# Output products of 128 tokens each, wider filler products, two subtractions moved to VectorE, and a new rank table

## The chip, the core and the metric

The kernel runs on one NeuronCore of a Trainium2 chip. The core has TensorE (PE in the profile; its weight loads are PEld), VectorE (DVE), ScalarE (ACT), GpSimd (POOL) and SyncE (SP), which here issues every transfer. The metric is the device time of one execution in microseconds (us), the median of several runs.

## The reference

Attention between 512 tokens and 32 state rows for 8 x 8 heads, then a gated feed-forward layer on 4352 tokens, then a soft mixture of experts over the same tokens.

```python
scores = scale * np.matmul(x, state.transpose(0, 1, 3, 2))     # x: (8, 8, 512, 64), state: (8, 8, 32, 64)
a = softmax(scores); xread = np.matmul(a, state)
a2 = softmax(scale * np.matmul(state, x.transpose(0, 1, 3, 2))); sread = np.matmul(a2, x)
t = np.concatenate([xread, sread], axis=2)                     # -> (4352, 512) tokens
h = t @ w_in; t = (h * sigmoid(h)) @ w_out                     # 512 -> 2048 -> 512
logits = t @ phi                                               # 32 slots = 8 experts x 4
d = softmax(logits, axis=0); slot_input = d.T @ t
slot_out[e] = np.maximum(slot_input[e] @ w1[e], 0) @ w2[e]     # 512 -> 1024 -> 512 per expert
out = softmax(logits, axis=1) @ slot_out                       # (4352, 32) @ (32, 512)
```

`moe_w_in` and `moe_w_out` arrive as 8-byte floats and are turned into 4-byte floats on the chip.

## The kernel before

The tokens are worked in nine blocks: k = 0 to 7 are the batches (512 tokens of `xread` each), k = 8 (`NB`) is the 256 tokens of `sread`.

The **front** loads `w_in` and `w_out` as sixteen 1 MB halves (`raw`), in the order of the list `RAW`. `conv` turns one half into 4-byte floats: ScalarE takes the high words (`win` or `acc`), ScalarE or, for the halves in `LOW_DVE`, VectorE the low words (`part`), VectorE shifts the high words, GpSimd adds the two. From `w_out` and `phi` the front makes `w2p` (`wo_half`: products `w2ps` and `w2q`). The attention of a block is `a_scores` (product `sc`), `a_split`, `a_soft1` to `a_soft3` (VectorE and ScalarE; from block 2 on GpSimd takes two of the steps), `a_eT` and `a_sread` (`sr`). `a_soft3` ends with `ar`, the attention weights split in a rounded part and a rest, so that fast products give the accuracy of 4-byte floats. `wb(u)` multiplies the state of a block with a quarter of `w_in` (u = 4 * block + quarter) and splits the result in the same way: ScalarE copies the rounded part, and the rest is a subtraction on VectorE, or, for one of its two halves (`WB_POOL`) when u > 3, on GpSimd after a second copy by ScalarE into `wf`.

For each block the **middle** runs `hid` sixteen times (product `h`, ScalarE's or VectorE's gate `g`, a transpose into `blk`), `logits` (`lg`), `s_rep`, `s_norm` and `s_dTg` (`S`), while the attention and the `wb` of later blocks run beside it. The **tail** multiplies the slots with `w_out` (`siaT`, `sia`, `sibT`, `sib`, `siT`), then with the experts' `w1` (`f`) and `w2` (`so`); both arrive in 32 transfers of 1 MB into places that earlier tiles leave. The output is made in two halves of 256 columns: `so` and `sor` of one half, then `out_tiles` for each block. `out_tiles(q, cols, tags)` runs 32 x 32 products of 256 columns (16 for a block of 512 tokens), four output banks with four token groups each; VectorE and ScalarE copy two banks each to `obuf`, and SP stores them (512 KB for a block and half). The first half of the output stands between the products `so` of the second half. Block 7 is made last, with 512 columns at once. A 4-byte product is two instructions on TensorE, each with its weight load.

The order is not that of the code. `Recorder` collects all operations (all have line 504 in the profile), and `schedule` simulates the engines with the costs of `cost`: on each engine it takes the operation that can start first, and among those that can start together the one with the smallest number, which is the position in the code plus an entry of `RANK`. A key of `RANK` is the zone ("0": all that stands ahead of block 1, "m": blocks 1 to 6, "7", "8"), the engine, the operation, the tile's name and a running number. Operations with `op.port` are not put beside each other on VectorE and GpSimd. All loads of the start are ready at once, so that their order is that of the numbers. The numbers of the code for these are: `raw` 0: 1, first state load `ss` 0: 2, `xT` 0: 3, `raw` 1: 4, `cst`: 5, `phi`: 6, `raw` 2: 7, `xk` 0: 8, second state load `ss` 1: 9, `raw` 3 to 7: 10 to 14. `raw` 0 and 1 are the two halves of the first quarter of `w_in`; `xT` 0, `xk` 0 and each `raw` are 1024 KB, `ss` 0 is 64 KB and `ss` 1 448 KB.

Where the simulation leaves TensorE idle in a stretch of `FILL`, `schedule` puts in products whose result nobody reads (`filler`); in the profile they carry the name of the tile whose bank they use, with both operands from `ss` (or `cst`), as `lg<-ss`.

Of the kernel before, what the change touches and what calls it, by code (L numbers as in the profile page):

```python
# [7 lines left out]
F32 = mybir.dt.float32  # L8
# [8 lines left out]
NSLOT = 32  # L17
# [24 lines left out]

EVICT = 100

FILL = ((0.0, 60.0), (380.0, 400.0))
FILLER = (0.47, 0.3)

HALVES = (0, 1, 2, 3, 4, 5, 6, NB)

# [3 lines left out]


RANK = {
    ("0", "ACT", "activation", "acc", 0): 54,
    ("0", "ACT", "activation", "acc", 4): -236,
    ("0", "ACT", "activation", "e", 1): -37,
    ("0", "ACT", "activation", "g", 5): 426,
    ("0", "ACT", "activation", "g", 6): 75,  # L60
    ("0", "ACT", "activation", "g", 10): 427,
    ("0", "ACT", "activation", "g", 14): 358,
    ("0", "ACT", "activation", "g", 15): 60,
    ("0", "ACT", "activation", "part", 3): -128,
    ("0", "ACT", "activation", "part", 7): 683,
    ("0", "ACT", "activation", "win", 0): -53,
    ("0", "ACT", "copy", "wb", 8): 61,
    ("0", "ACT", "copy", "ws", 2): 290,
    ("0", "DVE", "tensor_scalar", "acc", 1): -75,
    ("0", "DVE", "tensor_scalar", "acc", 2): -74,  # L70
    ("0", "DVE", "tensor_scalar", "asm", 2): -164,
    ("0", "DVE", "tensor_scalar", "part", 2): 96,
    ("0", "DVE", "tensor_scalar", "tm", 1): 25,
    ("0", "DVE", "tensor_scalar", "win", 1): -340,
    ("0", "DVE", "tensor_scalar", "win", 3): -51,
    ("0", "DVE", "tensor_scalar", "win", 4): -98,
    ("0", "DVE", "tensor_tensor", "s", 3): 343,
    ("0", "DVE", "tensor_tensor", "wb", 1): 659,
    ("0", "DVE", "tensor_tensor", "wb", 2): 26,
    ("0", "DVE", "tensor_tensor", "wb", 3): 120,  # L80
    ("0", "DVE", "tensor_tensor", "wb", 4): 132,
    ("0", "DVE", "transpose", "blk", 9): -82,
    ("0", "DVE", "transpose", "blk", 11): 399,
    ("0", "PE", "matmul", "h", 12): -436,
    ("0", "PE", "matmul", "wps", 3): 54,
    ("0", "SP", "dma_start", "cst", 0): 40,
    ("0", "SP", "dma_start", "phi", 0): 373,
    ("0", "SP", "dma_start", "raw", 1): -6,
    ("0", "SP", "dma_start", "raw", 2): 53,
    ("0", "SP", "dma_start", "raw", 4): -134,  # L90
    ("0", "SP", "dma_start", "raw", 6): 656,
    ("0", "SP", "dma_start", "ss", 0): -262,
    ("0", "SP", "dma_start", "ss", 1): 118,
    ("0", "SP", "dma_start", "xT", 0): -349,
    ("0", "SP", "dma_start", "xk", 0): 142,
    ("7", "ACT", "copy", "wb", 2): 68,
    ("7", "ACT", "copy", "wf", 1): 77,
    ("7", "DVE", "scalar_tensor_tensor", "g", 0): 253,
# [19 lines left out]
    ("8", "PE", "transpose", "hT", 2): -503,  # L118
    ("8", "PE", "transpose", "lT", 0): 485,
    ("8", "SP", "dma_start", "blk", 10): 66,  # L120
    ("m", "ACT", "activation", "e", 0): 327,
    ("m", "ACT", "activation", "e", 1): -87,
    ("m", "ACT", "activation", "s", 0): 433,
    ("m", "ACT", "activation", "sums", 0): 783,
    ("m", "ACT", "activation", "thb", 2): -393,
    ("m", "ACT", "copy", "e", 0): 449,
    ("m", "ACT", "copy", "wb", 3): 366,
    ("m", "DVE", "reduce_sum", "cm", 0): 365,
    ("m", "DVE", "tensor_copy", "acc", 2): -172,
    ("m", "DVE", "tensor_scalar", "cm", 0): 376,  # L130
    ("m", "PE", "matmul", "S", 0): -413,
    ("m", "PE", "matmul", "h", 11): 276,
    ("m", "PE", "matmul", "lg", 10): -96,
    ("m", "PE", "matmul", "wbp", 2): -647,
    ("m", "PE", "transpose", "eT", 1): 283,
    ("m", "PE", "transpose", "srT", 0): 248,
}

# [36 lines left out]
class Recorder:  # L175
# [90 lines left out]
    def cost(self, op, eng, what, outs, ins, kwargs):  # L266
# [11 lines left out]
        if eng == PE:  # L278
            lhs, rhs = kwargs.get("lhsT"), kwargs.get("rhs")
            if what == "transpose":  # L280
                op.mode, op.tail = FULL, 0.2
                op.cost += 0.11
                return
            rows, cols = list(lhs.ap)[0][1], n(lhs)
            op.mode = (128 if rows > 64 else 64 if rows > 32 else 32, 128 if cols > 64 else 64 if cols > 32 else 32)
            N = n(rhs)
            if op.mode == FULL:
                split = rhs.dtype == F32R
                op.cost += N / 2.4e3 + 0.0157 if split else max(0.2, 4 * N / 2.4e3 + (0.021 if N > 256 else 0.04))
                op.tail = 0.165  # L290
            else:
                tiles = (128 // op.mode[0]) * (128 // op.mode[1])
                m = 2 * len(op.calls)
                op.cost = max(m / tiles * 2 * N / 2.4e3, m * 0.0135) + (0.07 if tiles == 16 else 0.0068 * tiles - (0.02 if N == 128 else 0.0))
                op.tail = 0.165
        elif eng == ACT:
            f = kwargs.get("func")
            base = 0.833e-3 * most
            if f in (AF.Abs, AF.Sign, AF.Relu):
                lat = base + (0.26 if pin else 0.29)  # L300
            elif most == 1024 and outs[0].dtype == U32:
                lat = 1.256
            elif f == AF.Prelu:
                lat = 1.165
            elif len(ins) > 1:
                lat = base + (0.258 if pin else 0.285)
            else:
                lat = base + (0.16 if pin else 0.205)
            if kwargs.get("accum_out") is not None:
                op.cost, op.tail = lat + 0.096, 0.0  # L310
            else:
                op.cost, op.tail = lat - 0.105, 0.105
            op.mode = {AF.Exp: "e", AF.Silu: "s", AF.Tanh: "es"}.get(f)
        elif eng == DVE:
            sb = [kwargs[x] for x in ("in0", "in1") if x in kwargs and kwargs[x].space == bass.MemoryType.SB]
            fast = not pin and not pout and not strided and what in ("tensor_scalar", "tensor_copy")
            op.port = len(sb) > 1 or fast
            if what == "transpose":
                lat = 0.165 + most / 0.96e3
            elif what == "reciprocal":  # L320
                lat = 0.165 + max(0, most - 4) * 6.7e-3
            elif fast:
                lat = 0.262 + most / 1.92e3
            else:
                lat = (0.205 if pin and len(ins) > 2 else 0.155) + most / 0.96e3
            op.cost, op.tail = lat - 0.08, 0.0 if fast else 0.08
        elif eng == POOL:
            lat = 0.2 + most * 2.135e-3
            if most == 1024:
                lat = {F32R: 2.39, U32: 2.5}.get(outs[0].dtype, 1.94)  # L330
            op.cost, op.tail = lat - 0.042, 0.042
        else:
            b = 4
            for s, c in list(outs[0].ap):
                b *= c
            op.bytes = b
            op.cost = 0.42
# [19 lines left out]
    def schedule(self):  # L357
# [38 lines left out]
        while n_left:  # L396
# [42 lines left out]
                free[tag] = f  # L439
                qpos[tag] += 1  # L440
            if e == PE and any(lo < busy[PE] < hi for lo, hi in FILL):
                n = int((st - busy[PE] - 0.3) / FILLER[min(fills, 1)])
                room = []
                for tag in free:
                    if tag.split("_")[1] == "ps" and tag[0] != "h" and (tag[0] == "w" or busy[PE] < 100) and free[tag] and qpos[tag] < len(queue[tag]):
# [44 lines left out]
    def filler(self, name, old, n, start):  # L490


        op = Op()
        op.eng, op.kind, op.firsts, op.done, op.mode, op.start, op.cost = PE, "fill", [name], False, FULL, start, 0.2 * n
        out, v = self.tiles[name][:, 0:128], self.filling[start > 100]
        op.calls = [(self.tc.nc.tensor.matmul, (out,), dict(lhsT=v, rhs=v, start=True, stop=True))] * n
        op.prio, op.idx, op.tail, op.key, op.old = 0, 0, 0.0, None, old
        return op

    def issue(self):  # L500
# [39 lines left out]
def tile_state_attention_soft_moe(  # L540
# [40 lines left out]
    r4 = cst[:, 128:160]  # L581
    masks = cst[:, 256:258]
    ss = unit("ss", [2, 4 * NB * NSLOT], "ss")
    nc.filling = ss[:, 0, 0:128], ident
    st_sb = ss[:, 0, :].rearrange("p (b c n) -> p b c n", b=NB, c=4)
    srT = ss[:, 1, :].rearrange("p (c y x n) -> p c y x n", c=4, y=2, x=4)
    w2p = one.tile([128, 4, 4, NSLOT], F32, tag="w2p", name="w2p")
# [188 lines left out]
    def a_soft3(b):  # L776
# [2 lines left out]
        nc.vector.transpose(out=t, in_=s[:, 0].rearrange("p h t -> p (h t)"))  # L779
        at[b, "ar"] = a = unit("A", [2, 2, 512], f"ar{b}", F32R)  # L780
        nc.scalar.copy(out=a[:, 0], in_=s[:, 1])
        (nc.gpsimd if b else nc.vector).tensor_tensor(out=a[:, 1], in0=s[:, 1], in1=a[:, 0].bitcast(F32), op=ALU.subtract)

    def a_eT(b, h2):
        e = at[b, "e"]
# [33 lines left out]
    def wb_mm(u, cols, n):  # L819
# [13 lines left out]
        for h2 in range(2):  # L833
            q = p[h2][:, :n]
            nc.scalar.copy(out=w[:, 0, h2, cols], in_=q)
            on = nc.vector
            if h2 in WB_POOL and u > 3:
                q = rot.tile([128, 512], F32, tag="wf", name=f"wf{u}_{h2}", bufs=1)[:, :n]
                nc.scalar.copy(out=q, in_=p[h2][:, :n])
                on = nc.gpsimd  # L840
# [582 lines left out]
    def out_tiles(q, cols, tags):  # L1423
# [2 lines left out]
        p = [bank(t, f"o{q}_{cols.start}_{x}") for x, t in enumerate(tags)]  # L1426
        nt = ntok(q) // 128
        with nc.together():
            for y in range(nt):
                for x in range(4):  # L1430
                    m = NSLOT * (4 * q + y)
                    mm(
                        p[x][32 * y:32 * y + 32, :n],
                        lhsT=cT[32 * x:32 * x + 32, m:m + 32],
                        rhs=sor[32 * x:32 * x + 32, cols],
                        start=True,
                        stop=True,
                    )
        for x in range(4):
            r = slice(0, 32 * nt)  # L1440
            (nc.scalar.copy if x % 2 else nc.vector.tensor_copy)(out=obuf[q][r, x, cols], in_=p[x][r, :n])
# [91 lines left out]
```

## Time and profile before

| | before |
|---|---|
| median of 3 runs | 461.36 us (460.88 to 461.5) |
| the profiled execution | 460.03 us, of which its span 456.7 us |
| TensorE busy | 427.5 us, 94% of the span |
| VectorE, ScalarE, GpSimd busy | 311.5, 276.9, 136.7 us |
| granted TensorE clock, mean | 0.992 of full speed |
| the chain that ended last | 82% on TensorE |
| transferred | 92.23 MB, of these 12.06 MB written |

The span runs from the first to the last instruction; the 3.3 us between it and the time of the execution lie around it. Busy shares are means over the stages named above, which have different limits, so that each stage is read by itself: the transfers are at their full rate up to 50 us and again from about 360 us on, and TensorE is busy without a gap in between.

### The profile page before, as it was taken

The numbers are of one execution on the slowest core, as the hardware profiler recorded it, in microseconds if no ns is written. First come the engines' busy times: TensorE is split into PE (matmuls) and PEld (weight loads), VectorE is DVE, ScalarE is ACT, GpSimd is POOL, SyncE is SP. The second block draws the span as 40 slices with busy tenths as digits, with TensorE's granted clock in tenths as the row PEclk, the third lists the DMA queues.
The fourth block names the chain that finished last, engine by engine and source line by source line (L and its number), as shares of the span: only waits on it lengthen the run. The fifth ranks groups of instructions, "written<-read, shape, count | busy, mean of one in ns | idle before, by whom it ended". The sixth has DMA issues, their size and how long they took to land.

```text
span 456.7 us, 12765 instructions
## 1 busy us (share of the span) xinstructions
PE 427.5 (94%) x5584; PEld 272.8 (60%) x5584; DVE 311.5 (68%) x535; ACT 276.9 (61%) x492; POOL 136.7 (30%) x75
## 2 busy tenths in 40 slices
PE   4778999999999999999999999999999999899981
PEld 3555656747656764865775677477577785434430
DVE  2979988888687696788768769767874405212361
ACT  3988987756676495496758649566568423110261
POOL 0746777242133134124214313421146430000000
PEclk9899999999999999999999999999999999999998
DMA  8999931220502412141160223210395899999998
GB/s 323 426 419 385 359 108 72 93 78 30 218 4 93 151 82 95 46 187 25 71 231 3 93 99 134 95 46 3 109 368 204 331 383 423 414 425 427 399 341 284
DMA packets 22247, 92.23 MB, mean 202 GB/s; under 512 B 1712, under 2 KB 9776, under 8 KB 13744
## 3 DMA queue, kind: packets, MB, share of 16 engines
q1 hardware_dynamic: 22192, 91.43, 51.9%
q8 instruction: 43, 0.70, 0.6%
q14 instruction: 12, 0.10, 0.1%
HBM read 79.37 MB, written 12.06 MB: 200 GB/s over the span
## 4 chain that ended last, share of the span: by engine, by line
PE 82%; ACT 6%; DVE 5%; issue 2%; POOL 1%; DMA 1%; DVEq 0%; SPq 0%; ACTq 0%
PE h L504 41%; PE lg L504 8%; PE S L504 8%; PE wbp L504 6%; PE so L504 3%; PE f L504 3%; PE o L504 3%; PE sc L504 2%; PE sr L504 2%; ACT part L504 1%; PE eT L504 1%; DMA ss<-in_stT_dram 1%; ACT e L504 1%; PE dT L504 1%; ACT win L504 1%
## 5 line engine op out<-in xcount | busy, mean ns | idle before, releaser
L504 PE MATMUL h<-ar,wb 128*128 128x512 f32 x768 | 191.0, 400 | 2.5 <-ACT g L504 1.0
L504 PEld LDWEIGHTS h<-ar,wb 128*128 128x128 f32 x768 | 139.8, 188 | 46.7 <-issue 12.5
L504 DVE STREAM_TRANSPOSE blk<-g 128x512 f32<-128x512 f32 x128 | 88.4, 700 | 22.0 <-ACT g L504 21.6
L504 ACT ACTIVATE g<-h 128x512 f32<-128x512 f32 x100 | 59.5, 604 | 55.2 <-PE h L504 35.7
L504 POOL TENSOR_TENSOR wb<-wf,wb 128x512 fp32r<-128x512 f32 x28 | 37.2, 1328 | 143.2 <-ACT wf L504 87.9
L504 PEld LDWEIGHTS lg<-g,w2p 128*32 128x32 f32 x1152 | 29.2, 109 | 28.3 <-issue 14.8
L504 PE MATMUL lg<-g,w2p 128*32 128x128 f32 x1152 | 40.8, 276 | 0.5 <-ACT w2p L504 0.5
L504 PE MATMUL S<-blk,dT 32*32 32x512 f32 (+1 forms) x1040 | 38.5, 599 | 0.4 <-ACT dT L504 0.4
L504 ACT CAST wb<-wbp 128x512 fp32r<-128x512 f32 x64 | 35.5, 597 | 3.4 <-PE wbp L504 3.4
L504 PE MATMUL wbp<-win,ss 64*32 64x512 f32 x512 | 33.7, 606 | 3.2 <-POOL win L504 3.2
L504 POOL TENSOR_TENSOR s<-s,tm 128x1024 f32<-128x1024 f32 x12 | 23.3, 1938 | 28.6 <-DVE tm L504 17.8
L504 POOL TENSOR_TENSOR win<-win,part 128x1024 uint32<-128x1024 uint32 x8 | 20.9, 2614 | 24.8 <-DVE asm L504 16.3
L504 ACT ACT_TABLE_LOAD x21 | 26.9, 1283 | 1.1 <-PEq L1523 0.7
L504 DVE TENSOR_TENSOR wb<-wbp,wb 128x512 fp32r<-128x512 f32 x36 | 24.2, 676 | 2.5 <-ACT wb L504 2.4
L504 DVE SCALAR_TENSOR_TENSOR acc<-acc,m,S 128x512 f32<-128x512 f32 x28 | 19.2, 743 | 7.5 <-PE S L504 7.5
L504 POOL TENSOR_TENSOR wlo<-win,whi 128x1024 fp32r<-128x1024 f32 x8 | 19.0, 2392 | 13.3 <-ACT whi L504 13.3
L504 POOL TENSOR_TENSOR acc<-acc,part 128x1024 uint32<-128x1024 uint32 x8 | 19.5, 2435 | 7.4 <-DVE acc L504 4.9
L504 POOL TENSOR_TENSOR ar<-s,ar 128x1024 fp32r<-128x1024 f32 x7 | 16.8, 2407 | 14.8 <-ACT ar L504 14.8
L504 PE MATMUL h<-whi,rd 128*128 128x512 f32 x64 | 20.5, 401 | 0.0
L504 DVE SCALAR_TENSOR_TENSOR g<-thb,h 128x512 f32<-128x512 f32 x28 | 18.5, 674 | 1.8 <-ACT thb L504 1.8
L504 ACT ACTIVATE thb<-h 128x512 f32<-128x512 f32 x30 | 17.5, 601 | 3.3 <-PE h L504 2.8
L504 DVE TENSOR_REDUCE tm<-s 128x32 f32<-128x1024 f32 x16 | 19.2, 1198 | 0.4 <-ACT s L504 0.4
(161 smaller groups left out, 589.3 us busy)
## 6 DMA issues: line engine op xcount, KB each, us to landing
place<-in_w_dram SPq DMA_DIRECT2D x17, 1024.0 KB, 10.8
blk<-in_w_dram SPq DMA_DIRECT2D x13, 1024.0 KB, 10.0
xT<-in_xT_dram SPq DMA_DIRECT2D x8, 1024.0 KB, 5.0
raw<-in_w_in_dram SPq DMA_DIRECT2D x8, 1024.0 KB, 11.7
raw<-in_w_outT_dram SPq DMA_DIRECT2D x8, 1024.0 KB, 7.8
xk<-in_xk_dram SPq DMA_DIRECT2D x8, 1024.0 KB, 5.0
blk<-in_w_out_dram SPq DMA_DIRECT2D x6, 1024.0 KB, 4.8
out_dram<-place SPq DMA_DIRECT2D x10, 512.0 KB, 5.9
```

The source lines that it names most:

```text
L504: made = [call(*args, **kwargs) for call, args, kwargs in op.calls]
```

## The change

Five edits. (1) `out_tiles` makes each output bank with one product of up to 128 tokens in place of four of 32. (2) Fillers are 256 columns wide in place of 128, stand only in the first 60 us, and their number comes from another formula (2.2 us are taken off the first gap, 0.2 us off the others); both operands come from the first 256 columns of the state tile. (3) The rests of `wb` for u = 4 and 5, and the rest of `ar` for block 1, are subtracted by VectorE; the copies into `wf` of these two u fall away. (4) The planner's costs: a VectorE shift or scaling of 4-byte integers with a strided operand now counts as short and as a user of `op.port`; GpSimd's integer addition counts 2.4 us in place of 2.5. (5) `RANK` has new entries for the zones "0" and "m".

```diff
-FILL = ((0.0, 60.0), (380.0, 400.0))
-FILLER = (0.47, 0.3)
+FILL = ((0.0, 60.0),)
+FILLER = 0.45
...
 RANK = {
...
-    ("0", "SP", "dma_start", "cst", 0): 40,
-    ("0", "SP", "dma_start", "phi", 0): 373,
-    ("0", "SP", "dma_start", "raw", 1): -6,
-    ("0", "SP", "dma_start", "raw", 2): 53,
-    ("0", "SP", "dma_start", "raw", 4): -134,
-    ("0", "SP", "dma_start", "raw", 6): 656,
-    ("0", "SP", "dma_start", "ss", 0): -262,
-    ("0", "SP", "dma_start", "ss", 1): 118,
-    ("0", "SP", "dma_start", "xT", 0): -349,
-    ("0", "SP", "dma_start", "xk", 0): 142,
...
+    ("0", "SP", "dma_start", "cst", 0): 24,
+    ("0", "SP", "dma_start", "phi", 0): 842,
+    ("0", "SP", "dma_start", "raw", 1): -66,
+    ("0", "SP", "dma_start", "raw", 4): 408,
+    ("0", "SP", "dma_start", "raw", 6): 19,
+    ("0", "SP", "dma_start", "raw", 7): 17,
+    ("0", "SP", "dma_start", "xk", 0): 402,
...
-            fast = not pin and not pout and not strided and what in ("tensor_scalar", "tensor_copy")
+            low = strided and outs[0].dtype == U32
+            fast = not pin and not pout and (low or not strided) and what in ("tensor_scalar", "tensor_copy")
             op.port = len(sb) > 1 or fast
...
-                lat = {F32R: 2.39, U32: 2.5}.get(outs[0].dtype, 1.94)
+                lat = {F32R: 2.39, U32: 2.4}.get(outs[0].dtype, 1.94)
...
-                n = int((st - busy[PE] - 0.3) / FILLER[min(fills, 1)])
+                n = int((st - busy[PE] - (0.2 if fills else 2.2)) / FILLER)
...
-        out, v = self.tiles[name][:, 0:128], self.filling[start > 100]
-        op.calls = [(self.tc.nc.tensor.matmul, (out,), dict(lhsT=v, rhs=v, start=True, stop=True))] * n
+        out, v = self.tiles[name][:, 0:256], self.filling
+        op.calls = [(self.tc.nc.tensor.matmul, (out,), dict(lhsT=v[:, 0:128], rhs=v, start=True, stop=True))] * n
...
-    nc.filling = ss[:, 0, 0:128], ident
+    nc.filling = ss[:, 0, 0:256]
...
-        (nc.gpsimd if b else nc.vector).tensor_tensor(out=a[:, 1], in0=s[:, 1], in1=a[:, 0].bitcast(F32), op=ALU.subtract)
+        (nc.gpsimd if b > 1 else nc.vector).tensor_tensor(out=a[:, 1], in0=s[:, 1], in1=a[:, 0].bitcast(F32), op=ALU.subtract)
...
-            if h2 in WB_POOL and u > 3:
+            if h2 in WB_POOL and u > 5:
...
-            for y in range(nt):
-                for x in range(4):
-                    m = NSLOT * (4 * q + y)
-                    mm(
-                        p[x][32 * y:32 * y + 32, :n],
-                        lhsT=cT[32 * x:32 * x + 32, m:m + 32],
+            for x in range(4):
+                m = 4 * NSLOT * q
+                mm(
+                    p[x][0:32 * nt, :n],
+                    lhsT=cT[32 * x:32 * x + 32, m:m + 32 * nt],
```

## Rows read from the trace of the kernel before

**Rows 1.** The page: rate of transfers in 40 slices of 11.4 us; instruction loads (packets, MB).

```profile
GB/s 323 426 419 385 359 108 72 93 78 30 218 4 93 151 82 95 46 187 25 71 231 3 93 99 134 95 46 3 109 368 204 331 383 423 414 425 427 399 341 284
...
q8 instruction: 43, 0.70, 0.6%
```

**Rows 2.** Stretches: length, busy time of each engine, clock, transfer share, GB/s.

```profile
20.00:49.90 29.90, 25.58 (x265) 18.16 (x257) 27.11 (x35) 26.69 (x37) 17.65 (x7) 0.96 1.01 406
49.90:66.00 16.10, 15.62 (x140) 9.91 (x140) 14.46 (x21) 13.95 (x21) 12.67 (x5) 1.00 0.57 207
60.00:80.00 20.00, 19.57 (x218) 11.49 (x217) 17.61 (x20) 15.42 (x27) 14.31 (x7) 1.00 0.16 56
```

**Rows 3.** TensorE in order of time, 6 to 20 us: start, length, operation, idle before.

```profile
6.17 1.96 PE L504 MATMUL sc<-xT,ss 64*32 64x512 f32 x16 [6.17 <-DMA ss<-in_stT_dram]
...
18.56 1.70 PE L504 MATMUL wbp<-win,ss 64*32 64x512 f32 x16 [2.97 <-POOL win L504]
```

**Rows 4.** The chain that ended last, 0 to 66 us: start, length, piece.

```profile
11.19 0.60 DVE win L504
...
12.78 1.06 ACT win L504
...
14.54 1.15 ACT part L504
...
18.94 0.56 DVE win L504
...
20.63 2.79 DVE acc L504
...
31.78 2.18 issue
```

**Rows 5.** Operations by tile: VectorE on the low words; ns min/median/max, first and last.

```profile
L504 DVE TENSOR_SCALAR part<-raw x6: 676/2034/2870, 31.2 to 66.0; 128x1024 uint32<-128x1024 uint32 x6
```

**Rows 6.** Operations by tile: the subtractions that VectorE does already.

```profile
L504 DVE TENSOR_TENSOR wb<-wbp,wb x36: 645/680/692, 23.3 to 333.8; 128x512 fp32r<-128x512 f32 x36
...
L504 DVE TENSOR_TENSOR ar<-s,ar x1: 1211/1211/1211, 26.5 to 26.5; 128x1024 fp32r<-128x1024 f32 x1
```

**Rows 7.** The chain that ended last, 420 to 457 us.

```profile
424.09 0.66 PE o L504 x32
424.74 1.44 PE so L504 x24
...
430.96 0.68 issue
...
436.73 0.73 PE o L504 x16
...
440.80 1.05 issue
...
446.53 1.16 issue
...
448.89 0.67 DVE place L504
```

**Rows 8.** Stretches of the output phase, columns as in rows 2.

```profile
435.00:441.00 6.00, 5.05 (x176) 2.42 (x177) 4.00 (x12) 3.63 (x12) 0.00 (x0) 1.00 0.96 312
441.00:450.00 9.00, 5.35 (x146) 1.62 (x145) 4.81 (x12) 4.35 (x12) 0.00 (x0) 1.00 1.08 378
450.00:452.00 2.00, 0.00 (x0) 0.00 (x0) 0.16 (x1) 0.00 (x0) 0.00 (x0) 1.00 0.94 267
```

**Rows 9.** Weight loads in order of time: start, length of the group, operation.

```profile
421.92 0.24 PEld L504 LDWEIGHTS o<-thb,place 32*32 32x32 f32 x32 [0.92 <-DVE thb L504]
...
125.58 0.42 PEld L504 LDWEIGHTS dT<-cst,d 128*128 128x128 f32 x4 [0.84 <-ACT thb L504]
```

**Rows 10.** TensorE beside the fillers: the stretch after its longest idle time; 386 to 392 us.

```profile
19.00:22.00 3.00, 3.00 (x24) 1.81 (x9) 3.00 (x3) 2.58 (x4) 2.42 (x1) 0.50 1.01 415
...
389.14 0.67 PE L504 MATMUL sibT<-thb,r4e 64*32 64x128 f32 x32 [1.13 <-DVE fin L504]
```

## What the change should do to the time, before it is measured

> **What bounds the kernel now.** I read the slices of the page first. They show three stages. Up to about 57 us the transfers run at 323 to 426 GB/s, then they drop, and from the 33rd slice (365 us) on they are above 380 GB/s again until the output begins [rows 1]. Next come the stretches. Before 49.9 us TensorE is busy 25.58 of 29.9 us, a good part of it with fillers; ScalarE is busy 26.69 and VectorE 27.11 of the 29.9: the conversions and the first attention set the pace. From 49.9 to 66 us TensorE is busy 15.62 of 16.1, and so it stays to the tail [rows 2]. A microsecond won before 49.9 us is thus handed through whole, since block after block the rest hangs on TensorE; a microsecond won on another engine after 49.9 us is worth nothing. Third, the chain of waits in the front: the pieces I want are those in which VectorE works or waits for something that is not the attention itself [rows 4]. Last, the chain in the output phase, where TensorE's products `o` and `so` alternate and TensorE three times stands still with "issue", waiting for nothing that the profile shows [rows 7], and the transfer rate in the same microseconds [rows 8].
>
> **The output products.** A full tile is now 32 instructions and takes 0.66 us of the chain, a round of `so` with 24 instructions 1.44, that is 0.48 for the eight instructions of four products side by side [rows 7]. The new tile is eight instructions, four products side by side, each on its own 32 rows and into its own bank. I price it like `so`, at 0.48, since both stream 256 columns four at a time; 0.18 less for each of eight tiles is 1.4 us between the first `o` and the last `so`.
>
> The three "issue" pieces are 0.68, 1.05 and 1.16 us [rows 7]. I take them for instructions that come late: 43 loads carry TensorE's 11168 instructions [rows 1], 260 each. From the first output tile on TensorE works through 1024 instructions for `o` and 260 for `so` and `sor`, five loads; after the change 272 and 260, two loads, in much the same time. So I let all three go. Together the second half of the output can begin 1.4 + 0.7 = 2.1 us earlier and TensorE's last nine tiles, now 12.2 us from 436.73 to 448.89, take some 2.2 us less [rows 7].
>
> Little of these 4.3 us reaches the end, because what is late next is the store. From 441 to 450 us the stores run at 378 GB/s with the engines' share at 1.08, so they are full. Only from 435 to 441 us (312 GB/s) and 450 to 452 us (267 GB/s) do they fall short [rows 8]: (378 - 312) x 6 + (378 - 267) x 2 = 618 KB, which is 1.6 us at 378 GB/s. More than that can't come out of the tail while the weights' arrival stays where it is. I take all of it: **-1.6 us**; bounds 0 (the stores take back everything) and -2.1 (the weights' part too).
>
> **Against this: the weight loads.** The 32 small loads of a tile now lie within 0.24 us, while four loads of 128 columns take 0.42, 0.105 each [rows 9]. If the eight new loads can't overlap, they take 0.84 us, a tile costs about 0.84 + 0.2 = 1.04, and the tail loses more than the instruction loads give. I think they overlap, because the old ones do so over row groups and column groups alike. [...]
>
> **The front: order of loads.** By the numbers in the code and the new entries, `raw` 1 (4 - 66) and `raw` 0 now go ahead of `ss` 0 and `xT` 0, which have lost -262 and -349. Two more loads of 1 MB, 2.1 MB at 426 GB/s [rows 1], are 4.9 us: the first product `sc` moves from 6.17 to about 11.1 us, while the first `wbp`, which needs only these two halves and the state, moves from 18.56 to 12 to 15 us [rows 3]. The other loads that the table moves (`phi`, `raw` 4, `xk`) are used late, and SP does nothing else then.
>
> The attention chain starts 4.9 us later. In exchange the conversion of these two halves is out of its way: the pieces of 0.60, 1.06, 1.15 and 0.56 us on the chain, 3.4 us [rows 4]. The 2.79 us of `acc` at 20.63 is a 0.68 us operation (the shortest of its kind, [rows 5]) that stood waiting for GpSimd, as `part` does in most of its six places (median 2.03 us). The planner of before did not count these as users of the common port; the new one does and can put them elsewhere: 2.1 us. Sum: +4.9 - 3.4 - 2.1 = -0.6. The second such wait on the chain, 2.18 us at 31.78 [rows 4], is likewise avoidable; I count half, -1.1. Of the -1.7 I take **-1.0 us**, because ScalarE is already 89% busy in that stretch [rows 2] and shortens nothing by itself. Bounds: ScalarE's own idle time, 29.9 - 26.69 = 3.2 us, as the most that can be won; as the loss the whole 4.9 us if the chain keeps its pieces.
>
> **Block 1's rests.** VectorE gets two subtractions of 0.68 and one of 1.21 us [rows 6], 2.6 us, and ScalarE loses two copies. From 60 to 80 us VectorE has 20 - 17.61 = 2.4 us idle [rows 2], and the GpSimd work that it now waits for gets less; behind these subtractions VectorE has the transposes of `g` and the next `wb`, for which TensorE would wait. I take 0: TensorE is busy 19.57 of 20 there. Bounds -0.4 (its idle time) and +2.6 (no cover at all).
>
> **Fillers.** The new operands take in the columns of `ss` 1. With the new entries `ss` 1 is sixth, with 4.7 MB sent up to its end: 3.7 MB in the first slice and 1.0 at 426 GB/s, about 13.8 us. A filler right after `sc` (11.1 + 2.0) can wait for 0.7 us, with no real product behind it that matters to the chain. [...] I take 0; bounds -0.5 and +0.7.
>
> **Ranks of zone "m".** I can't work out the new order of blocks 1 to 6 from the table. A change of product shape costs 0.66 - 0.48 = 0.18 us [rows 7]; one more or one less in each of six blocks is 1.1 us either way. I take 0 and keep both ends.
>
> **Sum.** -1.6 - 1.0 = -2.6 us against the profiled execution: 460.03 - 2.6 = 457.4. Its time lies 1.3 us below the median of the three runs shown, 461.36, so the median to expect is **458.8 us**. About 0.2% (0.9 us) is what a measurement of this kernel can tell from no change.
>
> **Rivals.**
> *Only the tail gains.* What the new front wins on one engine it loses on the next: -1.6, 459.8 us. For it speaks that three engines are near full before 49.9 us. Chance 0.20.
> *The front gives all of ScalarE's idle time.* -1.6 - 3.2 = -4.8, 456.6 us. Against it: loads too are full until 50 us, and a half can't be converted before it lands. Chance 0.12.
> *No change.* The stores stay full at a lower rate once products come faster (312 GB/s may be the rate of first-half stores and not a lack of them), and the front is even: 461.4 us. Chance 0.12.
> *The attention comes late, and the kernel gets slower.* The place is the first `sc`, moved by 4.9 us. If other conversions fill the freed places in the chain (ScalarE and VectorE take what is ready), nothing of the 4.9 is caught up: +4.9 - 1.6 = +3.3, 464.7 us. It decides for slower from the point at which more than 2.5 us of the 4.9 stay. For it: `sc` is the first link of the chain today. Against it: the first two halves are needed for block 0 as well. Chance 0.12.
> *The weight loads of 128 columns stand in a row.* Eight tiles at 1.04 in place of 0.66 cost 3.0 us, less 0.68 of "issue", so the second half starts 2.3 us later; its nine tiles take about 10.5 in place of 12.2. The last copy comes 0.6 us later than now, and with an even front that is 462.0 us. Chance 0.04.
>
> My own case has 0.40, with a range of its own from 457.3 to 460.2 us. Adding up: faster 0.72 (own case, only the tail, the front's idle time), same 0.12, slower 0.16. For 8 in 10 the range reaches down past the 456.6 case by one switch per block (1.1 us), 455.5, and up into the late-attention case, 462.4.
>
> **What would show it.** Right: the products `o` come as eight instructions in about 0.5 us, the "issue" pieces of the output phase are gone, and the stores hold about 378 GB/s from the first second-half tile to the end; `sc` starts near 11 us and `wbp` before 15; VectorE's `part` and `acc` operations are mostly near 0.68 us; from 60 to 80 us TensorE has no new gaps. Wrong: `o` tiles of 0.8 us or more; the same 312 GB/s although the copies come early; the first `h` later than now by more than 2.5 us; TensorE gaps before `lg` or `S` of block 1 that end with VectorE; a clock below 1.00 in 380 to 400 us; or blocks 1 to 6 that differ in length by more than 0.2 us each.

## The result, and the profile after

The changed kernel takes **456.04 us** (median of 4 executions, 454.98 to 456.49) beside 461.12 us (459.51 to 461.50) of the kernel before: ratio 0.9893, 95% interval 0.9863 to 0.9924. Forecast were 458.8 us: the sign is right, the gain is 5.1 us in place of 2.6. The profiled execution took 456.44 us with a span of 454.6 us; before it was 460.03 with 456.7. So of 3.6 us in this pair 2.1 lie in the span and 1.5 around it.

To see where the 2.1 us come from I follow three products that both kernels make at the same place of the computation: the first `S` of block 1, the first `lg` of block 8 and the first `sor`; the `eT` shown ahead of them is used further below. TensorE in order of time (start, length, operation), before:

```profile
60.77 0.60 PE L504 MATMUL eT<-cst,e 128*128 128x128 f32 x4
...
130.88 1.14 PE L504 MATMUL S<-blk,dT 32*32 32x512 f32 x32
...
373.99 1.08 PE L504 MATMUL lg<-g,w2p 128*32 128x128 f32 x32
...
420.71 0.70 PE L504 MATMUL sor<-sos,cst 128*128 128x256 f32 x2 [0.49 <-ACT sos L504]
```

The same view of the kernel after, with its front and the products around `siT`:

```profile
11.70 1.96 PE L498 MATMUL sc<-xT,ss 64*32 64x512 f32 x16 [11.70 <-DMA xT<-in_xT_dram]
13.60 1.96 PE L498 MATMUL wbp<-win,ss 64*32 64x512 f32 x16
...
34.35 1.09 PE L498 MATMUL sc<-xT,ss 64*32 64x512 f32 x16 [1.01 <-DMA xT<-in_xT_dram]
...
59.76 0.60 PE L498 MATMUL eT<-cst,e 128*128 128x128 f32 x4
...
128.82 1.14 PE L498 MATMUL S<-blk,dT 32*32 32x512 f32 x32
...
372.20 1.08 PE L498 MATMUL lg<-g,w2p 128*32 128x128 f32 x32
...
387.34 0.67 PE L498 MATMUL sibT<-thb,r4e 64*32 64x128 f32 x32 [1.13 <-DVE fin L498]
...
393.14 1.08 PE L498 MATMUL siT<-cst,sis 128*128 128x32 f32 x8 [0.94 <-DVE sis L498]
394.65 0.62 PE L498 MATMUL f<-blk,siT 128*32 128x512 f32 x2 [0.43 <-issue]
...
396.47 1.13 PE L498 MATMUL f<-blk,siT 128*32 128x512 f32 x2
...
420.58 0.70 PE L498 MATMUL sor<-sos,cst 128*128 128x256 f32 x2 [0.49 <-ACT sos L498]
```

`S` comes 2.06 us earlier, `lg` 1.79, but `sor` only 0.13: between 372 and 420 us nearly the whole gain of the front is lost again. The `f` at 396.47 shows how: its two instructions last 1.13 us in place of 0.62. From `sor` to the end of the span it is 34.0 us, before 36.0. The stretches of the kernel after (columns as in [rows 2]):

```profile
60.00:80.00 20.00, 20.00 (x209) 12.74 (x208) 15.15 (x22) 15.02 (x26) 8.88 (x4) 1.00 0.16 53
395.00:399.00 4.00, 4.00 (x28) 1.32 (x24) 0.00 (x0) 0.00 (x0) 0.00 (x0) 0.57 1.02 420
422.00:435.00 13.00, 12.65 (x186) 5.85 (x182) 4.99 (x14) 4.67 (x15) 0.00 (x0) 1.00 1.02 384
435.00:441.00 6.00, 5.06 (x61) 2.40 (x62) 5.04 (x15) 4.16 (x14) 0.00 (x0) 1.00 0.94 301
441.00:450.00 9.00, 2.40 (x24) 0.77 (x24) 3.38 (x8) 2.94 (x8) 0.00 (x0) 0.81 1.07 363
```

From 395 to 399 us the granted clock is 0.57. From 60 to 80 us TensorE has no gap left and VectorE is busy 15.15 us, before 17.61. VectorE's low words no longer wait (operations by tile, min/median/max in ns):

```profile
L498 DVE TENSOR_SCALAR part<-raw x6: 649/679/686, 31.2 to 65.6; 128x1024 uint32<-128x1024 uint32 x6
```

Before, the four long ones of [rows 5] (31.17, 37.55, 47.71 and 59.88 us) stood beside an addition of GpSimd, and each ended about 0.55 us after that addition: GpSimd is what they waited for.

The chain in the output phase has no "issue" piece over 0.22 us any more, and the eight weight loads of a tile (second fence, start and length of the group) take 0.31 us:

```profile
421.80 0.71 PE o L498 x8
422.51 1.43 PE so L498 x24
423.94 0.64 PE o L498 x8
...
435.45 0.67 PE o L498 x8
...
443.63 0.67 DVE place L498
```

```profile
421.80 0.31 PEld L498 LDWEIGHTS o<-thb,place 32*128 32x128 f32 x8 [0.92 <-DVE thb L498]
```

An output tile is 0.64 us between two `so`, not 0.48 ([rows 7]: 0.66 before). Even so VectorE's last copy starts 23.0 us after `sor`, before 28.2: 5.1 us earlier, of which the end of the span takes over 2.0, because the stores behind it come last (from 450 to 452 us no engine is busy and the transfers run at 350 GB/s).

### The profile page after: what moved, and what is told of

It is laid out like the page before. It is cut to its first block, busy times and chain, and to the rows that moved or that the text cites. A ratio compares the mean times of both kernels' runs of the same rounds, so it can differ in the third digit from the quotient of the medians.

```text
span 454.6 us, 11912 instructions
## 1 busy us (share of the span) xinstructions
PE 422.4 (93%) x5156; PEld 269.5 (59%) x5156; DVE 302.1 (66%) x538; ACT 275.7 (61%) x490; POOL 129.2 (28%) x72
## 4 chain that ended last, share of the span: by engine, by line
PE 84%; DMA 7%; ACT 3%; DVE 2%; issue 1%; SPq 1%; DVEq 0%; ACTq 0%
PE h L498 43%; PE lg L498 8%; PE S L498 8%; PE wbp L498 6%; DMA xT<-in_xT_dram 4%; PE f L498 3%; PE so L498 3%; DMA raw<-in_w_in_dram 3%; PE o L498 2%; PE sc L498 2%; PE eT L498 1%; PE sr L498 1%; PE dT L498 1%; PE gt L498 1%; PE sib L498 1%; DVE place L498 1%
## 5 line engine op out<-in xcount | busy, mean ns | idle before, releaser
L498 POOL TENSOR_TENSOR wb<-wf,wb 128x512 fp32r<-128x512 f32 x26 | 34.0, 1309 | 136.9 <-ACT wf L498 103.8
L498 DVE TENSOR_TENSOR wb<-wbp,wb 128x512 fp32r<-128x512 f32 x38 | 25.4, 676 | 4.7 <-ACT wb L498 4.7
L498 POOL TENSOR_TENSOR win<-win,part 128x1024 uint32<-128x1024 uint32 x8 | 19.4, 2420 | 17.1 <-ACT part L498 7.5
L498 PE MATMUL sc<-xT,ss 64*32 64x512 f32 x128 | 9.6, 658 | 12.7 <-DMA xT<-in_xT_dram 12.7
L498 ACT COPY e<-eT 128x512 f32<-128x512 f32 x16 | 9.6, 600 | 18.2 <-PE eT L498 18.2
```

What stands on the lines that cost most here:

```text
L498: made = [call(*args, **kwargs) for call, args, kwargs in op.calls]
```

## The experiments

Open were five points: what the output products give by themselves; whether the fall of the clock costs what the marks say, and whether TensorE's idle time sets it off; what of the 2.06 us of the front is the order of the loads, what the port waits (VectorE's `part` and `acc` beside an addition of GpSimd, as in the four long `part` above) and what the rests; whether the rests cost nothing; and what shortens the time around the span. My theory: the front's gain is port waits and order, the tail's gain is missing instructions, and the fillers taken out near 390 us cost the clock. The rivals stand with each run. The marks of all profiled executions, in us; the first `eT` of block 1 is a further mark, behind the same products of TensorE in all (fillers aside; in b_port behind 64 more), and the third column is the time from it to `S`:

| kernel | first `eT` of block 1 | from it to `S` | first `S` of block 1 | first `sor` | span | median time |
|---|---|---|---|---|---|---|
| before | 60.77 | 70.11 | 130.88 | 420.71 | 456.7 | 461.12 |
| b_again | 60.85 | 70.15 | 131.00 | 420.83 | 456.8 | 460.11 |
| b_out | 61.18 | 70.12 | 131.30 | 421.01 | 455.7 | 457.69 |
| b_rests | 61.11 | 71.43 | 132.54 | 422.25 | 458.2 | 461.49 |
| b_port | 64.59 | 76.52 | 141.11 | 430.82 | 467.4 | 471.92 |
| after | 59.76 | 69.06 | 128.82 | 420.58 | 454.6 | 456.04 |
| a_again | 59.69 | 69.05 | 128.74 | 418.74 | 453.2 | 454.98 |
| a_fill | 59.27 | 69.03 | 128.30 | 418.38 | 453.2 | 454.85 |
| a_oldout | 59.19 | 69.04 | 128.23 | 418.25 | 454.9 | 457.04 |
| a_loads | 60.08 | 69.05 | 129.13 | 420.86 | 454.8 | 456.66 |
| a_rests | 59.67 | 69.99 | 129.66 | 419.76 | 454.6 | 456.16 |
| a_pool | 59.52 | 71.95 | 131.47 | 421.54 | 456.8 | 459.03 |
| a_blind | 61.27 | 75.18 | 136.45 | 426.50 | 460.5 | 464.63 |

Kernels that share a front show the scatter. The three with the old one (before, b_again, b_out) have `S` at 130.88 to 131.30 us, the four with the new one (after, a_again, a_fill, a_oldout) at 128.23 to 128.82. This comes in ahead of `eT`; from `eT` to `S` each group agrees within 0.04 us. So a difference of less than 0.6 us in `S` says nothing by itself, and the third column says more.

**The output products alone (b_out).** The kernel before with edit (1) only.

```diff
-            for y in range(nt):
-                for x in range(4):
...
+            for x in range(4):
+                m = 4 * NSLOT * q
+                mm(
+                    p[x][0:32 * nt, :n],
+                    lhsT=cT[32 * x:32 * x + 32, m:m + 32 * nt],
```

> The kernel before with the output products of 128 tokens alone. Theory T (the output phase is worth about 2 us, since the three instruction waits go and the stores are closed up): 1.5 to 2.2 us faster than before, with the span's start to the first output product unchanged within 0.1 us. Rival R (the stores take back everything, and the 2.0 us that the changed kernel gains behind its first output product come from elsewhere): within 0.5 us of before. If the 1.5 us by which the changed kernel's execution lies nearer to its span hang on the number of instructions (T2), this kernel's time exceeds its span by about 1.9 us in place of 3.3; if not, by 3.3.

Measured: 457.69 us against 460.79, ratio 0.9927 (0.9910 to 0.9944). These 3.1 us are more than either theory had. The median span is 455.7 us; on the same chip it is 457.4 in b_again and 457.8 in the executions of the kernel before that 460.79 is the median of. So 1.7 to 2.1 us lie in the span and about 1.1 around it. The "issue" pieces are gone, and the last copy starts 23.0 us after `sor`, as in the kernel after.

**The old output products in the kernel after (a_oldout).** The same edit, backwards.

> The changed kernel with the old output products of 32 tokens. Theory T: 1.5 to 2.2 us slower than the changed kernel, with instruction waits of 0.7 us and more back between the products o. Rival R: the same as the changed kernel within 0.5 us. The wait of the first products f at the lower clock stays in both.

Measured: 457.04 us, ratio 0.9913 (0.9895 to 0.9932). The "issue" waits are back (chain that ended last):

```profile
429.63 0.70 PE o L498 x24
430.33 1.45 issue
431.78 0.63 PE o L498 x8
...
440.86 0.69 issue
```

It is 1.0 us slower than the kernel after, less than theory T had. But the clock stayed at 1.00 from 395 to 399 us here, which was not expected, so that the partner is a_fill below, where it did too: median spans 455.25 and 453.1 us, medians of the time 2.2 us apart. The output products are worth 1.7 to 2.1 us in the span by the one pair and 2.1 by the other.

That these waits are for instructions is argued from the DMA queue that carries them, 16 KB at a time. In the kernel before such loads start at 421.8, 429.5, 434.2, 439.5 and 445.4 us, and the three waits end 2.2 to 2.3 us after the second, fourth and fifth. Here the waits end at 431.78 and 441.55, and over the span the queue carries 43 loads as in the kernel before. The kernel after has 40, two of them in that stretch, at 427.0 and 434.3, and no wait. Why some loads cost a wait and others none stays open.

**Three products put back near 390 us (a_fill).** The kernel after with fillers of 128 columns from 380 to 400 us: three products more on TensorE, all else unchanged.

```diff
-FILL = ((0.0, 60.0),)
+FILL = ((0.0, 60.0), (380.0, 400.0))
...
-        out, v = self.tiles[name][:, 0:256], self.filling
+        out, v = self.tiles[name][:, 0:128 if start > 100 else 256], self.filling[start > 100]
```

> The changed kernel with three filler products (128 columns) put back between sum and f, everything else in its order. Theory C (the removal of these fillers let the clock fall to 0.57 from 395 to 399 us, and the 1.7 us that TensorE loses there are on the path): the clock stays at 1.00, the first output product comes 1.5 to 1.8 us earlier, and the end as much. Rival D (the weights' transfers set the end of this stage, so TensorE's loss is hidden): the f products are at full speed, but the end moves by less than 0.4 us.

Measured: 454.85 us (454.66 to 455.13 in five executions), ratio 0.9867 (0.9848 to 0.9886). It beats both kernels. The fillers lie in the gaps (the second group is shown), and `f` keeps its 0.62 us (TensorE in order of time):

```profile
391.63 0.71 PE L498 MATMUL f<-cst 128*128 128x128 f32 x4
392.64 1.08 PE L498 MATMUL siT<-cst,sis 128*128 128x32 f32 x8 [0.30 <-DVE sis L498]
...
395.86 0.63 PE L498 MATMUL f<-blk,siT 128*32 128x512 f32 x2
```

From `lg` (371.67) to `sor` it is 46.71 us here, 46.72 before and 48.38 in the kernel after: the fall of the clock costs TensorE 1.67 us. Of theory C the product times came as expected; the end moved by 1.2 us, somewhat less than the 1.5 to 1.8. That it was the fillers which kept the clock up is not shown by this run alone, as the next one tells.

**The kernel after once more (a_again).** Unchanged.

> The kernel after, unchanged. Theory T1 (the clock's fall behind `f` is worth about 1.5 us and comes in most executions, not in all): median 455.7 to 456.3 us, with executions in two groups about 1.2 us apart, a mean clock near 0.987 in the slow group and 0.991 in the fast one. Rival T2 (what the three added products gave has nothing to do with the clock; the chip of that run was a quick one): all executions on this chip within 0.5 us of each other, whatever their clock.

Measured: 454.98, 456.07, 454.98, 456.29 and 454.46 us, on one chip and thus in two groups, with the profiled 454.98 at a clock of 1.00 from 395 to 399 us. With the four executions of the result there are nine: four at 454.5 to 455.0, mean clock 0.989 to 0.991, and five at 455.7 to 456.5, mean clock 0.987 to 0.988; the medians are 1.3 us apart. By the two profiled ones (one of each group) that is the fall; only they show where the clock fell, so that five of nine is read from time and mean clock. T2 is out, since the executions on this chip lie 1.8 us apart. But idle time alone does not decide the fall: the execution without it has the same waits,

```profile
392.99 1.08 PE L498 MATMUL siT<-cst,sis 128*128 128x32 f32 x8 [0.94 <-DVE sis L498]
394.50 0.62 PE L498 MATMUL f<-blk,siT 128*32 128x512 f32 x2 [0.43 <-issue]
```

and so has the profiled execution of a_oldout. Of the profiled executions without these fillers two show the fall behind `f` (after and a_loads) and five do not (a_again, a_oldout, a_rests, a_pool, a_blind); of the six with them (before, b_again, b_out, b_rests, b_port, a_fill) none does. None of six beside two of seven can be chance, the more so as a_fill ran on the chip of a_oldout, which kept its clock without them. The mean clock doesn't decide it for the other executions: it counts the idle end of the span too (0.50 from 450 to 452 us in the kernel after), and a_rests has 0.989 without the fall. So what the fall costs is shown, that the missing fillers cause it is not, and what tips it stays open.

**The kernel before once more (b_again).**

> The kernel before, unchanged, to see in several executions how far its time lies above its span. If the 3.3 us of the profiled execution are its own: 3.0 to 3.6 in most. If they vary from one execution to the next for any kernel: a spread of 1.5 us or more, reaching the 1.8 us of the changed kernel.

Measured: 460.11 us, ratio 0.9990 (0.9973 to 1.0006), with the "issue" pieces of 0.68, 1.05 and 1.16 us again: they belong to the program and not to one execution. The time lies 3.0 to 3.4 us above the span in nine of the twelve executions and 2.2 in three, never as little as the 1.8 us of the kernel after.

**The order of the loads (a_loads).** The kernel after with `ss` 0 and `xT` 0 sent first again; every engine's order is kept.

```diff
-        order = self.schedule()
+        order = sorted(self.schedule(), key=lambda o: o.key not in (("0", SP, "dma_start", "ss", 0), ("0", SP, "dma_start", "xT", 0)))
```

> The kernel after, with the first state load `ss` 0 and `xT` 0 sent first again, ahead of `raw` 1 and `raw` 0; every engine keeps its order. The two loads are 1.06 MB, about 2.6 us at 410 GB/s. Theory Q (the order of the loads gives the 2.0 us): `sc` starts near 6 us, the first `wbp` 2.5 us later than 13.6, the conversions behind it are pushed and the first `S` comes at 130.5 to 131.5, the time 1.7 to 2.6 us longer than after. Rival P (the port waits give it): what comes late at first is caught up by the attention that comes early, the first `S` within 0.6 us of 128.8.

Measured: 456.66 us, ratio 0.9915 (0.9897 to 0.9934). `sc` starts at 6.53 us, and the first `wbp` 3.2 us later than 13.60:

```profile
6.53 1.96 PE L498 MATMUL sc<-xT,ss 64*32 64x512 f32 x16 [6.53 <-DMA xT<-in_xT_dram]
16.83 1.96 PE L498 MATMUL wbp<-win,ss 64*32 64x512 f32 x16 [8.35 <-POOL win L498]
```

The first `S` comes only 0.31 us later, within the scatter, and from `eT` to `S` it is 69.05 us as in the kernel after. Theory Q is out: which load comes first is worth next to nothing in this order, since what the attention gains, the conversion loses.

**The rests, the rest of the order kept (a_rests, b_rests).** In the kernel after, the three subtractions of block 1 (three, not the two of the title) go to GpSimd (two behind a copy by ScalarE); in the kernel before they go to VectorE and the two copies fall away. No other instruction changes its place. The diff is that of a_rests; b_rests does the reverse, on VectorE and from the bank itself.

```diff
+        if b == 1:
+            nc.ops[-1].calls = [(tc.nc.gpsimd.tensor_tensor, (), nc.ops[-1].calls[0][2])]
...
+            if h2 in WB_POOL and u in (4, 5):
+                x = rot.tile([128, 512], F32, tag="wf", name=f"wf{u}_{h2}", bufs=1)
+                nc.ops[-1].calls = [
+                    (tc.nc.scalar.copy, (), dict(out=x, in_=q)),
+                    (tc.nc.gpsimd.tensor_tensor, (), dict(nc.ops[-1].calls[0][2], in0=x)),
+                ]
```

> The kernel after with every engine's order kept; the three subtractions of the second block alone go to GpSimd, the two of `wb` behind a copy by ScalarE into `wf`. Theory R1 (the cover that these edits need is there, so they are worth nothing; what the run planned anew lost, it lost because the table does not fit that plan): the first `S` of block 1 within 0.4 us of 128.8, the time within 0.6 us of that of the kernel after. Rival R2 (1.0 to 2.0 us of the front are theirs, since on GpSimd each rest comes later by about 0.6 to 1.2 us and TensorE's `h` of block 1 stand behind it): the first `S` at 129.8 to 131, the time 1 to 2 us longer.

> The kernel before with every engine's order kept; the same three subtractions alone go to VectorE, and the two copies into `wf` fall away. R1: the first `S` within 0.4 us of 130.9, the time that of the kernel before. R2: the first `S` at 129 to 130, the time 1 to 2 us shorter; TensorE busy from 60 to 80 us above 19.9 of 20. If VectorE has no cover for the 2.6 us (the other end that was predicted), the first `S` comes later than 131.3.

Measured: a_rests 456.16 us, ratio 0.9899 (0.9879 to 0.9919); `S` comes 0.84 us later than in the kernel after, and from `eT` to `S` it is 0.93 us more. That lies between R1 and R2, and the time, 0.1 us longer than after, can't tell them apart, since executions with and without the fall of the clock are mixed in it. One of TensorE's waits from 20 to 95 us (us, times, longest) is new there and names the rest of `ar`; none names the two of `wb`:

```profile
PE h L498 <- POOL ar L498: 0.7, 1, 0.7
```

b_rests 461.49 us, ratio 1.0026 (1.0009 to 1.0043): `S` comes 1.66 us *later* than before, of which 0.34 stand at `eT` already, where TensorE has not yet met the edit; from `eT` to `S` it is 1.32 us more. The stretch from 60 to 80 us, VectorE's low words, and what TensorE waits for:

```profile
60.00:80.00 20.00, 19.37 (x210) 10.44 (x208) 19.17 (x24) 14.03 (x23) 9.57 (x5) 1.00 0.17 61
```

```profile
L504 DVE TENSOR_SCALAR part<-raw x6: 681/1998/2861, 31.5 to 66.0; 128x1024 uint32<-128x1024 uint32 x6
```

```profile
77.53 2.17 PE L504 MATMUL wbp<-win,ss 64*32 64x512 f32 x16 [0.20 <-DVE wb L504]
```

VectorE is nearly full (19.17 of 20; 17.61 before), and a `wbp` that takes 1.09 us elsewhere takes 2.17: its banks are freed by the subtractions. This is the end of the expectation in which VectorE has no cover. So the same edit is worth +1.32 us in one order and -0.93 in the other. That the difference is VectorE's free time is argued from these rows: in the old order a low word still holds it for 2.0 us (median), in the new one for 0.68. The new order was also planned with these subtractions in it, and no run separates the two.

**Three that planned anew (a_pool, a_blind, b_port).** a_pool: the rests back on GpSimd, with the planner's own order. a_blind: the kernel after with `low = False`, so that the planner doesn't count VectorE's shifts of the low words as users of `op.port`. b_port: the kernel before with the two new costs (edit 4) alone.

> The kernel after, with the three subtractions of the second block back on GpSimd (and the two copies into `wf` back on ScalarE); planned anew with the table of the kernel after, so that places of other operations shift too. As predicted (the three edits are worth nothing, TensorE is the bound there): the first `S` within 0.5 us of 128.8, the time within 0.7 us of that of the kernel after. Rival R (the rests on VectorE free GpSimd and ScalarE in the front, and part of the 2.0 us is theirs): the first `S` at 129.8 to 131, the time 1 to 2 us longer. A table that doesn't fit the new plan would show as TensorE's idle time spread over several places, and leave this one unsettled.

> The kernel after, with the planner again blind to VectorE's use of the common port in the shifts of the low words; the order is planned anew and differs in the front alone. Theory P (the front's 2.0 us are port waits that the planner now avoids): `part` and `acc` on VectorE are again 2 us and longer in several places, the first `S` comes at 130 to 132 us in place of 128.82, the time is 1.2 to 3 us longer than that of the kernel after. Rival Q (the 2.0 us come from the order of the loads): one or two long `part`, off the chain, the first `S` within 0.5 us of 128.8, the time the same.

> The kernel before with the planner's two costs of the change alone (VectorE's strided shifts count as short and as users of the common port; GpSimd's addition 2.4 us); the order is planned anew with the table of the kernel before. Theory P (the port waits cost the front 1 to 3 us, and a planner that sees them wins that by itself): `part` and `acc` at 0.68 us, the first `S` at 128 to 130, the time 1 to 3 us shorter. Rival Q2 (a table searched for one plan does not fit another; the knowledge alone wins nothing, only costs and a new search together do): the waits are gone, but TensorE stands idle elsewhere, the first `S` at 131 or later, the time the same or longer.

Measured: a_pool 459.03 us, ratio 0.9962 (0.9944 to 0.9981); a_blind 464.63, ratio 1.0082 (1.0055 to 1.0109); b_port 471.92, ratio 1.0238 (1.0210 to 1.0265). a_pool does 2.65 us worse at the first `S` where the same edit in the kept order does 0.84 worse; the other 1.8 us are the misfit of order and table, and TensorE's new waits (w2ps 0.9, w2q 0.7, h 0.5 us) name none of the rests. b_port has its median `part` down from 2.03 to 0.68 us, as was wanted, and block 1's first `sc` comes at 34.05 us where it is at 36.18 to 36.59 in the three kernels with the old front: 2.1 to 2.5 us earlier, behind the same products of TensorE and with the loads in the old order. By `eT` this is gone, and from there to `S` it loses 6.4 us more, with a wait of 3.4 us for one `wb` among others. So up to `sc` the planner's costs alone win what was expected of the port waits, and the table, which was searched for another plan, loses far more behind that. a_blind does not test the port waits: its `part` keep a median of 0.68 us (longest 1.30), only one `acc` reaches 2.68, so that its 8.6 us say little about them.

## Why the prediction was right, and where its terms were off

The forecast came out in sign and in its main mechanisms, but the time itself came within the range partly by luck. It lies below the 457.3 to 460.2 us of my own case; the range reached down to 455.5 only by the switch in the middle, which measured nothing. And two terms of 1.3 us that the sum did not have, the time around the span and the fall of the clock, nearly cancel.

- **Middle, 0 +/- 1.1: right.** From the first `S` of block 1 to that of block 5 it is 154.2 us in both kernels (130.88 to 285.06 before, 128.82 to 283.06 after).
- **Output products, -1.6: right in mechanism and nearly in size.** 1.7 to 2.1 us (b_out) and 2.1 (a_oldout to a_fill) in the span; the stated most was 2.1. Five instruction loads before and two after stood in the forecast and came, and so did its main point, that TensorE's gain (4.3 forecast, 5.1 at the last copy) reaches the end only in part. The largest piece of that gain are the missing waits, 0.68 + 1.05 + 1.16 us of [rows 7]. What was wrong is the price of a tile: 0.48 us forecast, 0.64 measured, so that of 0.18 us a tile hardly 0.02 came. It was taken inside a run of `so`, and each `o` stands between `so` of another tiling. What the change of tiling costs by itself, no run separates. The rival of loads in a row is refuted (0.31 us for eight, not 0.84); the 0.2 us that it adds to them was an estimate that no run shows.
- **Stores at 378 GB/s to the end: not reached, and nearer without the fall of the clock.** From 435 to 441 us it is 301 GB/s in the kernel after and 357 in a_fill, where the second half starts at 433.25 us and not at 435.45; from 441 to 450 it is 363 and 369.
- **Front, -1.0: measured -2.06; the loads and the rests were mis-sized.** The loads moved as forecast (`sc` 11.70, forecast 11.1; `wbp` 13.60, forecast 12 to 15), but the +4.9 and -3.4 for them, +1.5 together, are nothing that a_loads can tell from the scatter. The port waits were forecast at -2.1 and half of a second 2.18 us; in b_port 2.1 to 2.5 us show at `sc`, but no run tells what of that is left in the new order. Up to the first `eT` of block 1 the pair gains 1.0 us, the size forecast, from terms that were not the forecast ones. The other 1.05 us come from `eT` to `S`, where the next point has them. That `part` and `acc` fall to 0.68 us was right: the median of `part` goes from 2.03 to 0.68 us, the longest from 2.87 to 0.69, and the longest of these `acc` from 2.90 to 0.77 (median 0.69 in both).
- **Rests, 0: measured -0.93 in the new order, and the bound of -0.4 was the wrong kind of bound.** It was TensorE's idle time in the order before; but the edit comes with an order in which VectorE is busy 2.5 us less from 60 to 80 us, these subtractions included. The loss that I bounded with +2.6 is real in the old order (+1.32). Without these subtractions the new order takes 69.99 us from `eT` to `S` (a_rests), the old one 70.11: so nearly all of the 1.05 us there is theirs.
- **Fillers, 0: this step failed.** No run shows the bound of -0.5. What shows is this: in the kernel before one wait of 2.97 us stands ahead of a clock of 0.50 from 19 to 22 us ([rows 3], [rows 10]); in the kernel after no wait from 380 to 400 us is longer than 1.13 us, but the clock falls in five of nine executions all the same, in the profiled one behind waits of 1.13, 0.94 and 0.43 us. It costs 1.67 us at `sor` and 1.3 us of the time; my bound was +0.7. The prediction had named "a clock below 1.00 in 380 to 400 us" as a sign of error, and it came. That the missing fillers bring it on is not shown (see a_again).
- **Time around the span: not in the sum.** Over 49 executions of the kernel before it is 2.2 to 3.8 us (median 3.1), over those of the kernel after and its six variants 1.73 to 1.86; the medians are 1.96 in b_out and 2.5 in b_port, which each take one part of the change. That is 1.3 us, a quarter of the gain. It is not the number of instructions: a_oldout has 12664 of them and 1.77 us, b_out 12013 and 1.96, before 12765 and 3.1. The cause stays open.

Added up for the profiled pair: -2.06 at the first `S`, +0.27 up to `lg`, +1.66 up to `sor` (the clock), -2.1 in the tail, -1.5 around the span: -3.6 us. The profiled execution without the fall of the clock (a_again) took 454.98 us, 5.1 below the 460.03 of the profiled execution before.

## What to carry to other kernels

A price for moving work to another engine holds only in the order in which it was read: the same three subtractions cost 1.32 us in one order and gave 0.93 in the other, so ask first how much time the receiving engine has *after* all other edits. A mark behind which kernels agree within 0.04 us (here from `eT` to `S`) tells such an edit's worth far better than the time of the whole. A product priced from a row inside a run of its kind was too cheap here, where it alternates with another tiling (0.48 us forecast, 0.64 measured). And gaps that are all shorter (1.13 us at most) than one that stood ahead of a fall of the clock (2.97 us) are no promise that it stays up: here the fall costs 1.3 us, in five of nine executions. The kernel with three small fillers back in them measured 0.8 us less (454.85 against 455.65, the median of the nine executions without them); whether the fillers did it needs more executions of both on one chip.

## What the hardware did that I had not expected

- TensorE's clock fell to 0.57 of full speed (the mean from 395 to 399 us) although no wait ahead of it from 380 us on was longer than 1.13 us, and did so, by time and mean clock, in five of nine executions of one program. The profiled executions of a_again and a_oldout, with the same waits of 0.94 and 0.43 us, did not show it.
- Waits for nothing that the profile shows, of 0.7 to 1.5 us, stand in the output phase where TensorE works through many short instructions while the transfers are full (engines' share 0.96 to 1.08 in [rows 8]), at the same places in two executions of the kernel before. In the profiled execution before, each ends 2.2 to 2.3 us after the start of an instruction load of 16 KB, while two other such loads there stand ahead of no such wait, and they went with three quarters of the instructions of the output tiles.
